# Dense + GELU, forward and backward, on one core: PSUM laid out by hand

## The chip, the cores and the metric

One Trainium2 chip, and of it one core. The metric is device time in microseconds of one execution, here of that core alone. The profiled execution is one run with the hardware profiler; its span runs from the first to the last instruction.

## The reference

```python
def _gelu(x): return jax.nn.gelu(x, approximate=True)
def _fwd_reference(x, w1, b1, w2, b2):         # x (1, 2048, 448), w1 (448, 1792), w2 (1792, 448), all bf16
    h = jnp.einsum("bsd,df->bsf", x, w1) + b1
    h = _gelu(h)
    return jnp.einsum("bsf,fd->bsd", h, w2) + b2
def reference(x, w1, b1, w2, b2, grad_out):
    _out, _vjp = jax.vjp(_fwd_reference, x, w1, b1, w2, b2)
    return (_out, *_vjp(grad_out))             # out, and the gradients of x, w1, b1, w2, b2
```

With u = x w1 + b1, h = gelu(u), q = grad_out w2^T and gh = q * gelu'(u), the six results are h w2 + b2, gh w1^T, x^T gh, the sum of gh over the rows, h^T grad_out, and the sum of grad_out over the rows.

## The kernel before

The 2048 rows are cut into NB = 4 blocks of SB = 512 rows, and the 1792 columns of the hidden layer into 14 f-tiles of 128, taken in NPAIR = 7 pairs. A step is one pair of f-tiles in one block, and there are NSTEP = 28. All of the order is written out by hand: inside `tc.manual_schedule()` every engine runs its instructions in the order of the program text, and the framework adds the semaphores and gives each tile its memory.

For a step f, TensorE computes u (transposed: 128 hidden columns by 512 rows) for the pair's two halves a = 0 and 1. Each half is three matmuls with 128 rows of contraction (`pe_u_fulls`, L201) and a "tail" with the 64 rows left over (`u_tail`, L217). `copy_u` (L256 on ScalarE, L258 on VectorE) adds the bias and copies each half from PSUM to the SBUF tile U4. Only the first, `copy_u(0, "av")`, splits the halves between ScalarE and VectorE; all others have both halves on ScalarE. Then follow, on 1024 columns of U4 at once, `act_gelu` (L262), `act_square` (L265), `dve_cubic` (L269, L270), `act_tanh` (L274) and `dve_gate` (L278 to L285). q of a step k is made in the same way (`q_tail` L224, then `pe_q_fulls` L247), and `dve_gh` (L290) multiplies it by the gate out of PSUM, both halves in one instruction.

What fills TensorE between u and q are "units": a unit is one tile of 128 rows of the output (kind "o", from hT) or of the gradient of x (kind "x", from ghT). A unit sums 7 pieces of two matmuls each (L322) in one PSUM bank, as far as the steps have come; `pieces(budget, ...)` issues them in the order in which units were opened. A finished unit is copied to a staging tile `st` (L333 on ScalarE or L335 on VectorE) and stored by GpSimd's queue (L336). There are STG = 5 staging tiles, so the sixth copy waits until the first store has landed.

The stages, in the order of time:

- steps 0 to 7, one at a time: u runs LEAD = 2 steps ahead of q. Four units are open from the start, a fifth and sixth from i = 6;
- steps 8 to 27, two at a time (the loop over n, nq = 10): u of steps k+2 and k+3, q of k and k+1, and one new unit (n < 2) or two (n from 2 to 8);
- the ten units that are left, in five pairs;
- the gradients of w1 (`ps_w`, L553 and L564) and of w2 (`ps_v`, L585), each a sum over 16 matmuls, with the sums for b1 and b2 on VectorE.

PSUM has eight banks of 512 floats per partition. The kernel before has two pools, psa and psb, each with two tiles of two banks that are given out in turn. In steps 0 to 7, u is always in one psa tile and q in the other (u of step 1 alone is where q comes next), and the units are in psb. From step 8 u has both psa tiles, q both psb tiles, and a unit takes half of one of these tiles, the other half being left empty:

```python
PU[f] = psa.tile([P, 2, SB], F32, name="pu", tag="pa")        # L198
in_a = k < NSINGLE or k >= NSTEP - 2                          # L211, NSINGLE = 8
PQ[k] = (psa if in_a else psb).tile([P, 2, SB], F32, name="pq", tag="pa" if in_a else "pb")
open_pair(psa, "pa", 1)                                       # L466, one unit in a psa tile
if n >= 2: open_pair(psb, "pb", 1)                            # L468, one unit in a psb tile
```

A tile is given out again when every access to the old one is over.

Of the kernel before, what the change touches and what calls it, by code (L numbers as in the profile page):

```python
# [9 lines left out]
ACT = mybir.ActivationFunctionType  # L10
# [9 lines left out]
def kernel(  # L20
# [42 lines left out]

    const = ctx.enter_context(tc.tile_pool(name="const", bufs=1))
    dram = ctx.enter_context(tc.tile_pool(name="dram", bufs=1, space=bass.MemoryType.DRAM))
    psa = ctx.enter_context(tc.tile_pool(name="psa", bufs=2, space=bass.MemoryType.PSUM))
    psb = ctx.enter_context(tc.tile_pool(name="psb", bufs=2, space=bass.MemoryType.PSUM))
    blk = ctx.enter_context(tc.tile_pool(name="blk", bufs=2))
    tmp = ctx.enter_context(tc.tile_pool(name="tmp", bufs=2))
    stg = ctx.enter_context(tc.tile_pool(name="stg", bufs=STG))  # L70
# [15 lines left out]
    gh_nat = const.tile([P, NB, NF, SPB, P], BF16, name="gh_nat")  # L86

    sched = ctx.enter_context(tc.manual_schedule())

    xT, gT = {}, {}  # L90

# [67 lines left out]
    nc.sync.dma_start_transpose(out=w1T_sb[:], in_=w1[:, :])  # L159
    load_g(1)  # L160

    pw = psb.tile([P, 2, SB], F32, name="pw", tag="pb")
    for i in range(9):
        nc.tensor.matmul(pw[:, 0, :], lhsT=zero[:, 0:P], rhs=zero[:], start=True, stop=True)
    for c in range(P // 32):
# [2 lines left out]

    hT, ghT = {}, {}
    PU, PQ = {}, {}  # L170
    U4 = [tmp.tile([P, 4, SB], BF16, name="U4", tag="U4", bufs=1)]
    A4 = [tmp.tile([P, 4, SB], BF16, name="A4", tag="A4", bufs=2) for _ in range(2)]
    Z4 = [tmp.tile([P, 4, SB], BF16, name="Z4", tag="Z4", bufs=1)]
# [20 lines left out]
    def pe_u_fulls(f):  # L194
        b, p = divmod(f, NPAIR)
        if p == 0:
            hT[b] = blk.tile([P, NF, SB], BF16, name="hT", tag="hT")
        PU[f] = psa.tile([P, 2, SB], F32, name="pu", tag="pa")  # L198
        for a in range(2):
            for kt in range(KF):  # L200
                nc.tensor.matmul(PU[f][:, a, :], lhsT=w1_f[:, kt, cols(p, a)], rhs=xT[b][:, kt, :], start=(kt == 0), stop=False,  # L201
                                 skip_group_check=True)

    def half(up):
# [2 lines left out]
    def open_q(k):  # L207
        b, p = divmod(k, NPAIR)
        if p == 0:
            ghT[b] = blk.tile([P, NF, SB], BF16, name="ghT", tag="ghT")  # L210
        in_a = k < NSINGLE or k >= NSTEP - 2  # L211
        PQ[k] = (psa if in_a else psb).tile([P, 2, SB], F32, name="pq", tag="pa" if in_a else "pb")

    def u_tail(f, a):
        b, p = divmod(f, NPAIR)
        hf = half(b not in WIDE)
        nc.tensor.matmul(PU[f][:, a, :], lhsT=wt1[hf, cols(p, a)], rhs=xT[b][hf, KF, :], start=False, stop=True,  # L217
                         tile_position=(hf.start, 0), skip_group_check=True)

    def q_tail(k, a, swap=False):  # L220
# [29 lines left out]
    def copy_u(f, engines):  # L250
        p = f % NPAIR
        for a in range(2):
            bias = b1T[:, 2 * FP[p] + a:2 * FP[p] + a + 1]
            dst = part(U4, [f])[:, a, :]
            if engines[a] == "a":
                nc.scalar.activation(out=dst, in_=PU[f][:, a, :], func=ACT.Identity, bias=bias)  # L256
            else:
                nc.vector.tensor_scalar(out=dst, in0=PU[f][:, a, :], scalar1=bias, scalar2=None, op0=ALU.add)  # L258

    def act_gelu(fs):  # L260
        for r in runs(fs):
# [47 lines left out]
    class Unit:  # L309
# [9 lines left out]
        def emit(self, p):  # L319
            src, w = (hT, w2_sb) if self.kind == "o" else (ghT, w1T_sb)  # L320
            for a in range(2):
                nc.tensor.matmul(self.ps[:, 0:D], lhsT=src[self.b][:, 2 * p + a, self.j * P:(self.j + 1) * P],  # L322
                                 rhs=w[:, 2 * FP[p] + a, :], start=(p == 0 and a == 0),
                                 stop=(p == NPAIR - 1 and a == 1 and not self.b2_pe), skip_group_check=True)
            if p == NPAIR - 1 and self.b2_pe:
                nc.tensor.matmul(self.ps[:, 0:D], lhsT=row0[:], rhs=b2_bc[:], start=False, stop=True, skip_group_check=True)
            self.done += 1

        def evict(self):
            st = stg.tile([P, SB], BF16, name="st", tag="st")  # L330
            r = ROW0[self.b] + self.j * P
            if self.by_act:
                nc.scalar.copy(out=st[:, 0:D], in_=self.ps[:, 0:D])  # L333
            else:
                nc.vector.tensor_tensor(out=st[:, 0:D], in0=self.ps[:, 0:D], in1=b2_bc[:], op=ALU.add)  # L335
            nc.gpsimd.dma_start(out=(out2 if self.kind == "o" else gx2)[r:r + P, :], in_=st[:, 0:D])  # L336

    todo = []
# [2 lines left out]
        todo += [Unit("x", b, j) for j in range(SPB)]  # L341
    open_units, finished = [], []

    def open_pair(pool, tag, n=2):
        t = pool.tile([P, 2, SB], F32, name="ps", tag=tag)
        for h in range(n):
            un = todo.pop(0)
            un.ps = t[:, h, :]
            open_units.append(un)

    def pieces(budget, fmax, gmax):
        for un in list(open_units):
# [43 lines left out]
    act_gelu([1])  # L396
    pe_u_fulls(2)
    pe_tails([2], [])
    open_pair(psb, "pb")
    open_pair(psb, "pb")  # L400
    pieces(4, 0, -1)
    pe_tails([], [0])
    pe_q_fulls(0)
# [8 lines left out]
    for i in range(1, NSINGLE):  # L412
        f = i + LEAD
        pe_u_fulls(f)
        pe_tails([f], [i])
        pe_q_fulls(i)
        if i > 1:
            act_tanh([i])
        evictions(2)
        copy_u(f, "aa")  # L420
        evictions()
        act_gelu([f])
        act_square([f])
        if i == 1:
            dve_gate([i])
            dve_cubic([i + 1])
        else:
            dve_cubic([i + 1])
            dve_gate([i])
        dve_gh(i)  # L430
        if i == 6:
            open_pair(psb, "pb")
        if i >= 5:
            stores(2, f - 1, i)
        traffic(i)
        pieces(7 if i >= 6 else 5, f - 1, i - 1)
# [3 lines left out]
    for n in range(nq):  # L440
        i = NSINGLE + n
        k = NSINGLE + 2 * n
        fs = [k + 2, k + 3] if k + 2 < NSTEP else []
        for f in fs:
            pe_u_fulls(f)
        pe_tails(fs, [k, k + 1])
        pe_q_fulls(k)
        pe_q_fulls(k + 1)
        if n == 0:
            evictions()  # L450
            act_tanh([k])
            for f in fs:
                copy_u(f, "aa")
            dve_gate([k])
            dve_cubic([k + 1])
            dve_gh(k)
            act_tanh([k + 1])
            dve_gate([k + 1])
            dve_gh(k + 1)
        else:  # L460
            for f in fs:
                copy_u(f, "aa")
            dve_gh(k)
            dve_gh(k + 1)
        if fs:
            open_pair(psa, "pa", 1)  # L466
            if n >= 2:
                open_pair(psb, "pb", 1)  # L468
            pieces(28, k + 1, k - 1)
            act_square(fs)  # L470
            if n < 2:
                evictions()
            act_gelu(fs)
            dve_cubic(fs)
            evictions(1)
            act_tanh(fs)
            dve_gate(fs, evictions)
        if i == 15:
            g_low = const.tile([P, SB], BF16, name="g_low")
            nc.gpsimd.dma_start(out=g_low[DL:P, :], in_=gT[3][0:DL, 0, :])  # L480
        stores(3, k + 1)
        traffic(i)
    stores(NSTEP, NSTEP - 1)
    flip = 1
    while todo:
        open_pair(psa if flip == 0 else psb, "pa" if flip == 0 else "pb")
        flip = 1 - flip
        pieces(28, NSTEP, NSTEP)
        evictions()

# [14 lines left out]
    for ft in range(4):  # L505
        load_h(ft)

    nev = [0]

    def gst(shape, f32src, dst, eng):  # L510
        st = stg.tile([P, SB], BF16, name="st", tag="st")
        return st

    def f_at(slot):
        return (2 * FP[slot // 2] + slot % 2) * P
# [31 lines left out]
                    nc.gpsimd.dma_start(out=v1[:, 0:2 * P], in_=gb1_w[0:1, F - 2 * P:F])  # L547

    def gw1_full(ft0, n, kt):
        ps = psb.tile([P, 2, SB], F32, name="ps_w", tag="pb")[:, 0, :]  # L550
        for st_ in range(NS):
            b, j = PLACE[st_]
            nc.tensor.matmul(ps[:, 0:n * P], lhsT=x_nat[:, st_, kt * P:(kt + 1) * P], rhs=gh_nat[:, b, ft0:ft0 + n, j, :],  # L553
                             start=(st_ == 0), stop=(st_ == NS - 1))
        o = stg.tile([P, SB], BF16, name="st", tag="st")
        nc.scalar.copy(out=o[:, 0:n * P], in_=ps[:, 0:n * P])
        nc.scalar.dma_start(out=out_2[kt * P:(kt + 1) * P, f_at(ft0):f_at(ft0) + n * P], in_=o[:, 0:n * P])

    def gw1_tail(ft0, n):
        ps = psb.tile([P, 2, SB], F32, name="ps_w", tag="pb")[:, 0, :]  # L560
        for st_ in range(NS):
            b, j = PLACE[st_]
            for h in range(2):
# [16 lines left out]
    def gw2_tile(ft, halves):  # L580
        w = D // halves
        for h in range(halves):
            ps = psa.tile([P, 2, SB], F32, name="ps_v", tag="pa")[:, 0, :]
            for st_ in range(NS):
                nc.tensor.matmul(ps[:, 0:w], lhsT=h_nat[ft][:, st_, :], rhs=g_nat[:, st_, h * w:(h + 1) * w],  # L585
                                 start=(st_ == 0), stop=(st_ == NS - 1))
            o = stg.tile([P, SB], BF16, name="st", tag="st")
            nc.scalar.copy(out=o[:, 0:w], in_=ps[:, 0:w])  # L588
            nc.scalar.dma_start(out=out_4[ft * P:(ft + 1) * P, h * w:(h + 1) * w], in_=o[:, 0:w])
# [44 lines left out]
```

## Time and profile before

| | |
|---|---|
| median of 3 runs | 278.41 us (276.49 to 278.45) |
| the profiled execution | 278.24 us, span 276.4 us, so 1.8 us lie around the span |
| mean granted TensorE clock | 0.999 |
| TensorE busy | 268.9 us (97%) |
| VectorE busy | 176.9 us (64%) |
| ScalarE busy | 138.8 us (50%) |
| GpSimd busy | 58.4 us (21%) |

The busy share of an engine is an average over stages with different limits, and the ends of matmuls are modelled, so a busy TensorE can still be one that has slack. "idle before, with a releaser" says what an engine waited for in front of an instruction. Names in the rows leave buffer numbers out: `pu` is u in PSUM, `U` the tile U4, `pq` is q in PSUM, `ps` a unit.

### The profile page before, as it was taken

What the parts mean: (1) busy time and instruction counts of PE and PEld (TensorE: products, weight loads), DVE (VectorE), ACT (ScalarE), POOL (GpSimd) and SP (SyncE); (2) the same over time, 40 slices, a digit from 0 to 9 for tenths busy, and PEclk for the clock granted to TensorE, in tenths of its full rate; (3) what the DMA queues carried; (4) which work ended last, traced back from release to release, by engine and by line L of the source; (5) the groups of instructions that cost most, each with busy time, mean ns of one, the idle gap of its engine ahead of it and who ended that gap; (6) DMA issues with size and microseconds to landing.
All of it is one profiled execution on the core that took longest, in us unless ns stands there. A gap on an engine that the chain in (4) does not pass through costs nothing.

```text
span 276.4 us, 3637 instructions
## 1 busy us (share of the span) xinstructions
PE 268.9 (97%) x1405; PEld 127.1 (46%) x1405; DVE 176.9 (64%) x213; ACT 138.8 (50%) x164; POOL 58.4 (21%) x77
## 2 busy tenths in 40 slices
PE   7999999999799999999999999999999999999995
PEld 2234434444344344444444445554444475555554
DVE  2388989969999997696977960207999993000000
ACT  2499979877898749696585901012111111112111
POOL 1000002542040221302114041311340006910000
PEclk9999999999999999999999999999999999999999
DMA  8999799999999954542445569998110111899951
GB/s 188 221 223 230 122 249 212 115 265 185 143 249 250 220 113 125 153 92 96 94 122 125 136 196 290 369 201 205 40 41 25 41 56 24 188 199 227 222 128 33
DMA packets 107521, 44.31 MB, mean 160 GB/s; under 512 B 91984, under 2 KB 104608, under 8 KB 107504
## 3 DMA queue, kind: packets, MB, share of 16 engines
q1 hardware_dynamic: 98224, 28.86, 55.0%
q0 software_dynamic: 4032, 11.55, 13.8%
q10 hardware_dynamic: 5248, 3.67, 4.4%
q8 instruction: 11, 0.18, 0.3%
q14 instruction: 6, 0.05, 0.1%
HBM read 7.23 MB, written 14.23 MB: 78 GB/s over the span
## 4 chain that ended last, share of the span: by engine, by line
PE 74%; DVE 14%; ACT 7%; DMA 2%; issue 2%; DVEq 0%
PE ps L322 24%; PE ps_v L585 15%; PE ps_w L553 13%; PE pq L247 8%; PE pu L201 8%; DVE ghT L290 3%; PE pu L217 3%; ACT U L256 2%; PE ps_w L564 2%; DVE Z L270 2%; ACT A L265 2%; DVE A L280 2%; DMA xT<-in_x_dram 2%; ACT hT L262 2%; DVE Z L285 2%
## 5 line engine op out<-in xcount | busy, mean ns | idle before, releaser
L256 ACT ACTIVATE U<-pu,b1T 128x512 bf16<-128x512 f32 x55 | 33.8, 685 | 26.7 <-PE pu L217 26.7
L322 PE MATMUL ps<-w1T_sb,ghT 128*128 128x448 bf16 x224 | 43.8, 352 | 1.6 <-ACT U L256 1.6
L322 PE MATMUL ps<-w_sb,hT 128*128 128x448 bf16 x224 | 44.8, 353 | 0.1
L585 PE MATMUL ps_v<-g_nat,h_nat 128*128 128x448 bf16 (+1 forms) x240 | 42.6, 340 | 0.0
L201 PE MATMUL pu<-xT,w_f 128*128 128x512 bf16 x168 | 40.6, 388 | 0.8 <-DMA xT<-in_x_dram 0.8
L290 DVE SCALAR_TENSOR_TENSOR ghT<-Z,pq 128x1024 bf16<-128x1024 bf16 x28 | 33.9, 1220 | 10.7 <-PE pq L247 9.2
L247 PE MATMUL pq<-gT,w2T 128*128 128x512 bf16 x168 | 39.4, 380 | 0.0
L336 POOL DMA_DIRECT2D out_dram<-st x32 | 18.2, 572 | 97.3 <-ACT st L333 50.0
L553 PE MATMUL ps_w<-gh_nat,x_nat 128*128 128x512 bf16 (+1 forms) x192 | 36.7, 352 | 0.0
L322 PEld LDWEIGHTS <-ghT 128*128 128x128 bf16 x224 | 21.9, 98 | 22.7 <-issue 1.9
L585 PEld LDWEIGHTS <-h_nat 128*128 128x128 bf16 x240 | 23.3, 98 | 19.3 <-issue 0.3
L322 PEld LDWEIGHTS <-hT 128*128 128x128 bf16 x224 | 21.8, 98 | 21.5 <-ACT hT L262 1.0
L274 ACT ACTIVATE Z<-Z 128x1024 bf16<-128x1024 bf16 (+1 forms) x19 | 27.7, 1457 | 6.6 <-DVE Z L270 6.6
L539 DVE TENSOR_TENSOR acc<-acc,gh_nat 128x1792 f32<-128x1792 f32 x14 | 30.0, 2142 | 0.5
L299 POOL DMA_DIRECT2D hT_dram<-hT x28 | 20.2, 726 | 46.5 <-DVE Z L269 44.6
L265 ACT ACTIVATE A<-U 128x1024 bf16<-128x1024 bf16 (+1 forms) x19 | 27.7, 1455 | 1.1 <-DVE U L258 0.8
L262 ACT ACTIVATE hT<-U 128x1024 bf16<-128x1024 bf16 (+1 forms) x20 | 27.7, 1391 | 0.2
L553 PEld LDWEIGHTS <-x_nat 128*128 128x128 bf16 x192 | 18.7, 98 | 17.8 <-issue 0.4
L201 PEld LDWEIGHTS <-w_f 128*128 128x128 bf16 x168 | 16.5, 99 | 21.7 <-issue 3.9
L247 PEld LDWEIGHTS <-w2T 128*128 128x128 bf16 x168 | 15.0, 98 | 23.2 <-issue 7.6
L588 ACT CAST st<-ps_v 128x448 bf16<-128x448 f32 (+1 forms) x15 | 7.6, 507 | 34.8 <-PE ps_v L585 34.8
L333 ACT CAST st<-ps 128x448 bf16<-128x448 f32 x20 | 10.0, 527 | 29.1 <-PE ps L322 28.0
(46 smaller groups left out, 204.2 us busy)
## 6 DMA issues: line engine op xcount, KB each, us to landing
hT_dram<-hT POOLq DMA_DIRECT2D x28, 256.0 KB, 4.1
out_dram<-st POOLq DMA_DIRECT2D x32, 112.0 KB, 4.3
x_nat<-in_x_dram SPq DMA_DIRECT2D x1, 1792.0 KB, 8.6
g_nat<-in_grad_out_dram SPq DMA_DIRECT2D x1, 1792.0 KB, 13.6
out_dram<-st ACTq DMA_DIRECT2D x13, 112.0 KB, 3.3
out_dram<-st ACTq DMA_DIRECT2D x9, 128.0 KB, 1.7
w_sb<-in_w_dram SPq DMA_DIRECT2D x5, 224.0 KB, 3.9
w_f<-in_w_dram SPq DMA_DIRECT2D x5, 192.0 KB, 4.1
```

The source lines that it names most:

```text
L201: nc.tensor.matmul(PU[f][:, a, :], lhsT=w1_f[:, kt, cols(p, a)], rhs=xT[b][:, kt, :], start=(kt == 0), stop=False, skip_group_check=True)
L247: nc.tensor.matmul(PQ[k][:, a, :], lhsT=w2T[:, kt, cols(p, a)], rhs=gT[b][:, kt, :], start=False, stop=(kt == KF), skip_group_check=True)
L256: nc.scalar.activation(out=dst, in_=PU[f][:, a, :], func=ACT.Identity, bias=bias)
L262: nc.scalar.activation(out=rows(hT, r), in_=part(U4, r), func=ACT.Gelu_apprx_tanh)
L265: nc.scalar.activation(out=part(A4, ks), in_=part(U4, ks), func=ACT.Square, scale=math.sqrt(3.0 * GELU_A * GELU_C))
L274: nc.scalar.activation(out=z, in_=z, func=ACT.Tanh, scale=-1.0 / 3.0)
L290: gates[k] = nc.vector.scalar_tensor_tensor(out=rows(ghT, [k]), in0=part(Z4, [k]), scalar=1.0, in1=PQ[k][:], op0=ALU.add, op1=ALU.mult)
L299: st = nc.gpsimd.dma_start(out=hT_dram_v[:, 2 * FP[p]:2 * FP[p] + 2, ROW0[b]:ROW0[b] + SB], in_=rows(hT, [f]))
L322: nc.tensor.matmul(self.ps[:, 0:D], lhsT=src[self.b][:, 2 * p + a, self.j * P:(self.j + 1) * P], rhs=w[:, 2 * FP[p] + a, :], start=(p == 0 ...
L539: nc.vector.tensor_tensor(out=v, in0=in0, in1=gh_nat[:, b, :, j, :], op=ALU.add)
L553: nc.tensor.matmul(ps[:, 0:n * P], lhsT=x_nat[:, st_, kt * P:(kt + 1) * P], rhs=gh_nat[:, b, ft0:ft0 + n, j, :], start=(st_ == 0), stop=(s ...
L585: nc.tensor.matmul(ps[:, 0:w], lhsT=h_nat[ft][:, st_, :], rhs=g_nat[:, st_, h * w:(h + 1) * w], start=(st_ == 0), stop=(st_ == NS - 1))
```

## The change

The two pools become one pool with eight banks under names of their own. `one_bank(n)` gives one of four single-bank tiles; `two_banks(n)` gives one of two tiles of two banks. The two halves of u are now two separate tiles. In steps 0 to 9 they have the banks 0 and 1 (step 1: 2 and 3). From step 10 the list `order_a` says which two banks the even step and which two the odd step takes. A unit that is opened beside u gets the bank `order_a[0]`, that of the first half of the even step, and the list is turned by one. q has `two_banks(0)` in steps 0 to 7 and after that the two tiles in turn (`order_b`); the second unit of n = 2 to 7 takes half of the tile that `order_b[0]` names, as before. At n = 8 the second unit is in a single bank, and q of steps 26 and 27 stays in the two-bank tiles. Units 2 and 3 have the single banks 2 and 3, behind u of step 1. The ten last units are in the four single banks. `ps_w` alternates between the two-bank tiles, and `ps_v` goes through the four single banks. No arithmetic is changed, and no instruction but for its tile.

```diff
-    psa = ctx.enter_context(tc.tile_pool(name="psa", bufs=2, space=bass.MemoryType.PSUM))
-    psb = ctx.enter_context(tc.tile_pool(name="psb", bufs=2, space=bass.MemoryType.PSUM))
+    psum = ctx.enter_context(tc.tile_pool(name="psum", bufs=1, space=bass.MemoryType.PSUM))
+    def one_bank(n, name):
+        return psum.tile([P, SB], F32, name=name, tag=f"one{n}")
+    def two_banks(n, name):
+        return psum.tile([P, 2, SB], F32, name=name, tag=f"two{n}")
...
-    pw = psb.tile([P, 2, SB], F32, name="pw", tag="pb")
+    pw = two_banks(1, "pw")
+    order_a, order_b = [0, 1, 2, 3], [0, 1]
...
-        PU[f] = psa.tile([P, 2, SB], F32, name="pu", tag="pa")
+        banks = (2, 3) if f == 1 else (0, 1) if f < NSINGLE + LEAD else order_a[2 * (f % 2):2 * (f % 2) + 2]
+        PU[f] = [one_bank(n, "pu") for n in banks]
         for a in range(2):
             for kt in range(KF):
-                nc.tensor.matmul(PU[f][:, a, :], ...
+                nc.tensor.matmul(PU[f][a][:], ...
...
-        in_a = k < NSINGLE or k >= NSTEP - 2
-        PQ[k] = (psa if in_a else psb).tile([P, 2, SB], F32, name="pq", tag="pa" if in_a else "pb")
+        PQ[k] = two_banks(0 if k < NSINGLE else order_b[k % 2], "pq")
...
-                nc.scalar.activation(out=dst, in_=PU[f][:, a, :], func=ACT.Identity, bias=bias)
+                nc.scalar.activation(out=dst, in_=PU[f][a][:], func=ACT.Identity, bias=bias)
             else:
-                nc.vector.tensor_scalar(out=dst, in0=PU[f][:, a, :], scalar1=bias, ...
+                nc.vector.tensor_scalar(out=dst, in0=PU[f][a][:], scalar1=bias, ...
...
+    def open_one():
+        open_unit(one_bank(order_a[0], "ps")[:, 0:D])
+        order_a.append(order_a.pop(0))
+    def open_two(n, units):
+        t = two_banks(n, "ps")
+        for h in range(units):
+            open_unit(t[:, h, 0:D])
...
-    open_pair(psb, "pb")
-    open_pair(psb, "pb")
+    open_two(1, 2)
+    for n in (2, 3):
+        open_unit(one_bank(n, "ps")[:, 0:D])
...
         if i == 6:
-            open_pair(psb, "pb")
+            open_two(1, 2)
...
-            open_pair(psa, "pa", 1)
-            if n >= 2:
-                open_pair(psb, "pb", 1)
+            open_one()
+            if n == nq - 2:
+                open_one()
+            elif n >= 2:
+                open_two(order_b[0], 1)
+                order_b.reverse()
...
     while todo:
-        open_pair(psa if flip == 0 else psb, "pa" if flip == 0 else "pb")
-        flip = 1 - flip
+        open_one()
+        open_one()
...
+    def bank_w():
+        flips[0] += 1
+        return two_banks(flips[0] % 2, "ps_w")[:, 0, :]
+    def bank_v():
+        order_a.append(order_a.pop(0))
+        return one_bank(order_a[-1], "ps_v")
```

More of the change, by code (lines that the diff above doesn't have):

```diff
@@ L197, in pe_u_fulls @@
             hT[b] = blk.tile([P, NF, SB], BF16, name="hT", tag="hT")
-        PU[f] = psa.tile([P, 2, SB], F32, name="pu", tag="pa")
+        banks = (2, 3) if f == 1 else (0, 1) if f < NSINGLE + LEAD else order_a[2 * (f % 2):2 * (f % 2) + 2]
+        PU[f] = [one_bank(n, "pu") for n in banks]
         for a in range(2):
             for kt in range(KF):
-                nc.tensor.matmul(PU[f][:, a, :], lhsT=w1_f[:, kt, cols(p, a)], rhs=xT[b][:, kt, :], start=(kt == 0), stop=False,
+                nc.tensor.matmul(PU[f][a][:], lhsT=w1_f[:, kt, cols(p, a)], rhs=xT[b][:, kt, :], start=(kt == 0), stop=False,
                                  skip_group_check=True)
@@ L216, in u_tail @@
         hf = half(b not in WIDE)
-        nc.tensor.matmul(PU[f][:, a, :], lhsT=wt1[hf, cols(p, a)], rhs=xT[b][hf, KF, :], start=False, stop=True,
+        nc.tensor.matmul(PU[f][a][:], lhsT=wt1[hf, cols(p, a)], rhs=xT[b][hf, KF, :], start=False, stop=True,
                          tile_position=(hf.start, 0), skip_group_check=True)
@@ L255, in copy_u @@
             if engines[a] == "a":
-                nc.scalar.activation(out=dst, in_=PU[f][:, a, :], func=ACT.Identity, bias=bias)
+                nc.scalar.activation(out=dst, in_=PU[f][a][:], func=ACT.Identity, bias=bias)
             else:
-                nc.vector.tensor_scalar(out=dst, in0=PU[f][:, a, :], scalar1=bias, scalar2=None, op0=ALU.add)
+                nc.vector.tensor_scalar(out=dst, in0=PU[f][a][:], scalar1=bias, scalar2=None, op0=ALU.add)
     def act_gelu(fs):
@@ L321, in emit @@
             for a in range(2):
-                nc.tensor.matmul(self.ps[:, 0:D], lhsT=src[self.b][:, 2 * p + a, self.j * P:(self.j + 1) * P],
+                nc.tensor.matmul(self.ps, lhsT=src[self.b][:, 2 * p + a, self.j * P:(self.j + 1) * P],
                                  rhs=w[:, 2 * FP[p] + a, :], start=(p == 0 and a == 0),
@@ L325, in emit @@
             if p == NPAIR - 1 and self.b2_pe:
-                nc.tensor.matmul(self.ps[:, 0:D], lhsT=row0[:], rhs=b2_bc[:], start=False, stop=True, skip_group_check=True)
+                nc.tensor.matmul(self.ps, lhsT=row0[:], rhs=b2_bc[:], start=False, stop=True, skip_group_check=True)
             self.done += 1
@@ L332, in evict @@
             if self.by_act:
-                nc.scalar.copy(out=st[:, 0:D], in_=self.ps[:, 0:D])
+                nc.scalar.copy(out=st[:, 0:D], in_=self.ps)
             else:
-                nc.vector.tensor_tensor(out=st[:, 0:D], in0=self.ps[:, 0:D], in1=b2_bc[:], op=ALU.add)
+                nc.vector.tensor_tensor(out=st[:, 0:D], in0=self.ps, in1=b2_bc[:], op=ALU.add)
             nc.gpsimd.dma_start(out=(out2 if self.kind == "o" else gx2)[r:r + P, :], in_=st[:, 0:D])
@@ L342, with open_unit @@
     open_units, finished = [], []
[L344 to L349, printed above, removed]
+    def open_unit(ps):
+        un = todo.pop(0)
+        un.ps = ps
+        open_units.append(un)
+    def open_one():
[5 more added lines that the diff above has]
+            open_unit(t[:, h, 0:D])
     def pieces(budget, fmax, gmax):
@@ L483 @@
     stores(NSTEP, NSTEP - 1)
-    flip = 1
     while todo:
-        open_pair(psa if flip == 0 else psb, "pa" if flip == 0 else "pb")
-        flip = 1 - flip
+        open_one()
+        open_one()
         pieces(28, NSTEP, NSTEP)
@@ L506 @@
         load_h(ft)
[L508 to L512, printed above, removed]
+    flips = [0]
+    def bank_w():
[4 more added lines that the diff above has]
+        return one_bank(order_a[-1], "ps_v")
     def f_at(slot):
@@ L549, in gw1_full @@
     def gw1_full(ft0, n, kt):
-        ps = psb.tile([P, 2, SB], F32, name="ps_w", tag="pb")[:, 0, :]
+        ps = bank_w()
         for st_ in range(NS):
@@ L559, in gw1_tail @@
     def gw1_tail(ft0, n):
-        ps = psb.tile([P, 2, SB], F32, name="ps_w", tag="pb")[:, 0, :]
+        ps = bank_w()
         for st_ in range(NS):
@@ L582, in gw2_tile @@
         for h in range(halves):
-            ps = psa.tile([P, 2, SB], F32, name="ps_v", tag="pa")[:, 0, :]
+            ps = bank_v()
             for st_ in range(NS):
```

## The prediction

> **What bounds the kernel now.** I read first the busy time by stage, then the chain of work that ended last, then TensorE's waits, then the timelines of ScalarE and VectorE at the places where the chain changes engine. The table by stage (window, length, then busy us of PE, PEld, DVE, ACT and POOL, clock, DMA share, GB/s):
>
> ```profile
> 25.00:40.40 15.40, 15.35 (x76) 6.17 (x75) 14.42 (x24) 13.51 (x16) 0.00 (x0) 1.00 0.94 190
> 59.60:92.20 32.60, 30.63 (x156) 13.47 (x152) 30.21 (x37) 26.18 (x26) 8.07 (x12) 1.00 1.19 206
> 92.20:161.80 69.60, 69.60 (x360) 31.90 (x360) 57.90 (x64) 50.28 (x49) 18.21 (x29) 1.00 0.51 124
> 161.80:188.30 26.50, 26.50 (x141) 13.70 (x140) 4.06 (x7) 1.94 (x5) 5.32 (x10) 1.00 1.05 280
> ```
>
> From 92.2 us on TensorE has no gap at all: matmuls of 512 columns follow each other at 0.216 us (12 in 2.59) and of 448 columns at 0.189 us (28 in 5.30), at a clock of 1.00. A new PSUM layout cannot shorten that; the end is the time at which TensorE gets going at 92.2, plus 184 us. So the question is what sets 92.2. The chain:
>
> ```profile
> 59.42 0.23 PE pu L217
> ...
> 59.67 0.45 ACT U L256
> ...
> 62.12 0.70 DVE Z L270
> ...
> 91.52 0.63 DVE st L335
> 92.15 0.04 issue
> 92.19 0.37 PE pq L224
> ```
>
> q of step 15 waits at 92.19 for VectorE to copy out a unit. VectorE reaches that copy after 30.2 busy us in the 32.6 from 59.6 on, in its own order: from 62.12 it has hardly a gap. 62.12 follows from ScalarE's four copies of u (steps 10 and 11), these from ScalarE's tanh and TensorE's u at 59.6. TensorE has run without a gap there since 40.41, when `dve_gh` of step 4 (39.13 to 40.35) freed q's only tile. And `dve_gh` ends a VectorE chain (14.42 of 15.40 us busy) that goes back to 24.95, where VectorE waited for ScalarE's square. From there back to the first copies of u at 9.7 the chain is ScalarE's, with short pieces of VectorE in it. So 9.7 to 25 is ScalarE's, 25 to 40 VectorE's, 40 to 59 TensorE's, 62 to 92 VectorE's. TensorE's own waits are few:
>
> ```profile
> PE ps L322 <- ACT U L256: 1.6, 1, 1.6
> PE pq L224 <- ACT U L256: 0.6, 1, 0.6
> PE pq L224 <- DVE st L335: 0.3, 1, 0.3
> ```
>
> **Part 1: the halves of u become tiles of their own.** The rows that decide are at the start:
>
> ```profile
> 8.65 1.03 PE L217 MATMUL pu<-xT,wt 64*128 64x512 bf16 x2
> 9.71 0.69 ACT L256 ACTIVATE U<-pu,b1T 128x512 bf16<-128x512 f32 x1 [6.42 <-PE pu L217]
> 10.43 0.75 DVE L258 TENSOR_SCALAR U<-pu,b1T 128x512 bf16<-128x512 f32 x1 [3.54 <-ACT U L256]
> 11.22 1.06 ACT L265 ACTIVATE A<-U 128x1024 bf16<-128x1024 bf16 x1 [0.82 <-DVE U L258]
> ```
>
> VectorE's copy of half 1 needs nothing of ScalarE's copy of half 0, yet waits for it, and ScalarE's begins only when both tails are over (9.68). Later copies show the same: at step 4 the tails start at 25.46 and 25.68, the second ends at 25.68 + 0.38 = 26.06, and the copy of half 0 starts at 26.10. So a wait holds for the whole two-bank tile, and with two tiles it goes: ScalarE can copy after the first tail, VectorE at 9.71 beside it, ending at 10.46 instead of 11.18. The square starts 0.72 earlier, and all of ScalarE's chain behind it. Bounds: 0 if VectorE still waits, 0.72 if the two read side by side at the durations above. For the latter: ScalarE's four copies at 91.75, beside a VectorE copy out of PSUM, took 2.42 us, against 2.40 at 72.00 without one. I take 0.72.
>
> The Trainium skill bears on this: page "PSUM — Partial Sum Buffer", section "PSUM bank collisions raise a hardware error", says that two engines on one bank collide, readers too, while different banks run clean. By that rule the two copies may overlap, which agrees with the 2.42 us beside 2.40; if two banks collided as well, they would have to stay in turn and the sum below would lose its 0.72.
>
> Does the 0.72 survive? VectorE at 24.95 waited 0.90 us for the square, so it follows. From 25 to 55 it is limited by itself and by q's tile, whose number is unchanged; the weights it needs come in time (the last transposes of the first block are issued at 21.56 and take 7.0 us to land, needed at 35). `dve_gh` of step 4 then ends at 39.6 and TensorE's stretch of 40 to 59 moves along.
>
> At 56 to 60 there is a second limit:
>
> ```profile
> 58.13 0.53 ACT L333 CAST st<-ps 128x448 bf16<-128x448 f32 x1 [1.05 <-DMA out_dram<-st]
> 58.55 1.06 ACT L274 ACTIVATE Z<-Z 128x1024 bf16<-128x1024 bf16 x1
> 59.67 2.42 ACT L256 ACTIVATE U<-pu,b1T 128x512 bf16<-128x512 f32 x4
> ```
>
> The sixth unit's copy waits for the store of the first (issued by GpSimd from 48.08 on, up to 10.3 us to landing, DMA engines saturated), the tanh is queued behind it on ScalarE, and the copies of u behind the tanh. The store is issued behind `dve_gh` of step 5, so its issue moves by 0.72 too; its landing moves by 0 (if the other transfers set it) to 0.72. In the first case the tanh still ends at 59.61 and the copies come only 0.05 earlier; at best they start when the first tail is over, 59.03 + 0.39 - 0.72 = 58.70, 0.95 earlier. Since GpSimd's queue is issued in order and moves as a whole, I take 0.7. VectorE's 62.12 moves by this, and with it 92.19.
>
> **Part 2: the unit in the bank of half 0.** At 71.66 TensorE waits 1.64 us for both copies of step 12 (ScalarE, four copies from 72.00 at 0.6 each: the second ends at 73.2). With a bank of its own the unit waits for one copy, and starts 0.6 earlier. But what is late next is the copy at 91.52, and VectorE does not get there sooner by it: TensorE would wait 0.6 longer at q of step 15, which has the same tile as before. Worth 0; worth 0.6 if VectorE were free. The next u needs the unit's bank only as its last half, 3 matmuls (0.65 us) later than before: slack only.
>
> **Part 3: units 2 and 3 behind u of step 1.** This adds a wait. Their first pieces, 4 matmuls of 0.19, ran at 13.5 to 15.1, ahead of the copies of step 1 (14.55 to 15.70), and q of step 0 waited for the copies at 15.76. Now the second and third pair of pieces wait for a copy each, and the tails and fulls of q (step 0) and all else on TensorE are queued behind: 2 x 0.19 = 0.38 us later against the copies. Cover: TensorE waits again 0.2 us at 17.8, VectorE has 0.90 us free at 24.95. Cost 0; 0.38 if that cover is gone. Since the copies come 0.72 earlier, q comes 0.34 earlier in all.
>
> **Part 4: the rest.** q of steps 26 and 27 now waits for `dve_gh` of 24 and 25, over at 154.5, and is due at 158.47: 4 us of cover. `ps_w` alternates as before; `ps_v` has four banks instead of two, but TensorE never waits there. A wait that is already met costs TensorE nothing that the rows show: u of two steps with two waits takes 12 x 0.216 + 0.10 = 2.69 us up to its tails, of one step with one wait 6 x 0.216 + 0.10 = 1.39. Instructions removed or added: none on the engines.
>
> **Sum**, against the profiled execution: 276.4 span + 1.84 around = 278.24; less 0.7 (Part 1), 0 (Parts 2 to 4) = **277.5 us**. That execution is within 0.2 us of the median of the runs shown, 278.41.
>
> **The rivals.**
> (A) *The store does not land earlier.* For: the DMA share is 1.17 from 40.4 to 59.6. Against: its issue is tied to VectorE. Then 278.24 - 0.05 = 278.2.
> (B) *The copies still take turns*, or slow each other down: the change does not do what it allows. For: nothing but that no row shows a ScalarE and a VectorE copy of one u side by side. With Part 3's 0.38 uncovered it would be 278.24 to 278.6.
> (C) *TensorE loses nearly all its waits for PSUM.* 1.64 + 0.59 at 15.76 + 0.33 at 92.19, and some 0.3 at 40.4, are 2.9: 275.3. The Trainium skill, page "Perfetto Trace Analysis", sections "Matmuls" and "Matmul Optimizations", says to rotate groups through different banks and to use all eight, which this change does where half-tiles stood empty. Against: 92.19 hangs on VectorE's 30.2 busy us, which no bank takes away.
> (D) *Slower: the last ten units run on two pairs of banks* instead of four tiles. A pair takes 5.3 us of TensorE; it is copied out right after (VectorE 172.41 and 177.76, ScalarE 167.11), and its banks are due again 5.3 us after its end, so 4 us are free. It decides once a copy is held by its staging tile for over 4 us: five tiles at 2 per 5.3 us tolerate stores of some 10.6 - 0.8 + 4 = 14 us to landing. The median there is 4.3 us, the longest of all stores 10.3, the DMA share 1.05. At 15 us and over, each of three pairs would wait 1 us or more: 278.24 + 3 = 281.2.
>
> **How the numbers follow.** Forecast 0.50; A 0.26; B 0.08; C 0.08; D 0.08. A measurement of this kernel can tell about 1% (2.8 us) from no change, and only C (faster) and D (slower) go beyond it: 0.08 faster, 0.84 within, 0.08 slower. The range leaves out C and D (0.16): its low end is the best of Part 1, 278.24 - 0.95 = 277.3, less 1.3 for the spread of the runs, whose lowest is 1.75 below this execution, so 276.0; its high end is B's 278.6 plus 0.3, 278.9.
>
> **What would show it.** Right: VectorE's first copy starts at about 9.7 beside ScalarE's, the first square at 10.5, `dve_gh` of step 4 ends near 39.6, the copies of step 10 start near 58.9, TensorE waits over 1 us at q of step 15, near 91.5, and then has no gap. TensorE's wait for a copy near 71 is about 1 us or less. Wrong: a VectorE wait that is gone between 62 and 92 (C), gaps of TensorE after 162 (D), or the sixth unit's copy still at 58.1 (A).

## The result, and the profile after

| | before | after |
|---|---|---|
| median of 22 runs each, on the same chip | 276.63 us (276.28 to 278.52) | **275.38 us** (275.05 to 277.52) |
| ratio after to before, 95% interval | | **0.9964** (0.9948 to 0.9979) |
| lower level: runs, median | 18, 276.53 us | 16, 275.33 us |
| upper level: runs, median | 4, 278.43 us | 6, 277.13 us |
| the profiled execution: time, span | 278.24, 276.4 us | 275.37, 273.6 us |

The change makes the kernel faster by 0.4%: 1.2 us at the lower level, 1.3 at the upper. The times of both kernels lie at two levels, 1.8 to 1.9 us apart, with nothing between them. Ratios and their intervals, here and below, are taken over the runs of both levels, which widens the intervals. The profiled execution of before is one of the upper level and that of after one of the lower, so their difference of 2.87 us is not what the change is worth. In what follows, times of a kernel are medians of its lower level unless something else is said.

The levels first, since every time stamp depends on them. The first lines of TensorE's timeline, before and then after (start and duration in us, the engine, the line, the operation, its tiles, how many):

```profile
1.18 4.02 PE L164 MATMUL pw<-zero 128*128 128x512 bf16 x9 [1.18 <-DVE zero L130]
6.00 2.72 PE L201 MATMUL pu<-xT,w_f 128*128 128x512 bf16 x6 [0.80 <-DMA xT<-in_x_dram]
...
9.61 1.47 PE L201 MATMUL pu<-xT,w_f 128*128 128x512 bf16 x6
```

```profile
1.18 3.99 PE L169 MATMUL pw<-zero 128*128 128x512 bf16 x9 [1.18 <-DVE zero L135]
6.05 1.46 PE L208 MATMUL pu<-xT,w_f 128*128 128x512 bf16 x6 [0.88 <-DMA xT<-in_x_dram]
7.43 0.60 PE L223 MATMUL pu<-xT,wt 64*128 64x512 bf16 x2
```

Both run nine idle matmuls at about 0.45 us each while they wait for x. After them the first u of the profiled run before still goes at 0.45 us per matmul (2.72 for six; the u of step 1, at 9.61, takes 1.47), that of after at 0.24. The granted clock in the table by stage reads 1.00 there in both, so the durations alone show it. The second tail is over at 9.68 in the one and at 8.03 in the other. Everything later hangs on that moment, so I call it E and compare the two traces relative to it:

| us after E | before | after | difference |
|---|---|---|---|
| first square (ScalarE) | 1.54 | 0.89 | -0.65 |
| copies of u of step 10 (ScalarE) | 49.99 | 49.05 | -0.94 |
| q of step 15 goes on (TensorE) | 82.51 | 81.33 | -1.18 |
| end of the span | 266.72 | 265.57 | -1.15 |

Of the 2.8 us between the spans, 1.65 are E and 1.15 are the change; the levels of the table above give 1.2 for the latter.

**The start.** From the timelines of ScalarE and VectorE of after:

```profile
7.86 0.69 ACT L262 ACTIVATE U<-pu,b1T 128x512 bf16<-128x512 f32 x1 [4.56 <-PE pu L223]
8.07 0.75 DVE L264 TENSOR_SCALAR U<-pu,b1T 128x512 bf16<-128x512 f32 x1 [1.14 <-PE pu L223]
8.92 1.06 ACT L271 ACTIVATE A<-U 128x1024 bf16<-128x1024 bf16 x1 [0.37 <-DVE U L264]
```

The two copies stand side by side, at the durations they had one after the other. ScalarE's begins at 7.86, after the first tail and before the second is over; VectorE's is released by TensorE (L223), no longer by ScalarE.

**Steps 10 and 11.** ScalarE's timeline of after:

```profile
54.17 0.97 ACT L339 CAST st<-ps 128x448 bf16<-128x448 f32 x2 [0.97 <-PE ps L328]
55.02 1.07 ACT L280 ACTIVATE Z<-Z 128x1024 bf16<-128x1024 bf16 x1
57.08 2.42 ACT L262 ACTIVATE U<-pu,b1T 128x512 bf16<-128x512 f32 x4 [0.99 <-PE pu L223]
```

Before, the fifth and the sixth unit's copies were 1.59 us apart, the tanh ended at 59.61 and the copies of u began at once. Now the two copies of units stand together, and ScalarE is idle for 0.99 us in front of the copies of u, which TensorE releases. That the two copies of units stand together is not the change's doing (see "The landing of the first store").

**The end of VectorE's stretch.** The chain of work that ended last, of after, then TensorE's waits for PSUM (in total, times, longest):

```profile
57.08 0.45 ACT U L262
...
59.53 0.69 DVE Z L276
...
88.69 0.63 DVE st L341
89.32 0.04 issue
89.36 0.37 PE pq L230
```

```profile
PE pq L230 <- DVE st L341: 0.8, 1, 0.8
PE ps L328 <- ACT U L262: 0.6, 1, 0.6
```

q of step 15 still waits for VectorE's copy-out, now 0.76 us where it was 0.33; in exchange the wait for copies of u near 70 is 0.6 instead of 1.64. Behind 89.36 TensorE has no gap, as before behind 92.19:

```profile
59.60:92.20 32.60, 31.23 (x155) 13.72 (x154) 31.03 (x36) 27.27 (x25) 8.67 (x12) 1.00 1.11 209
92.20:161.80 69.60, 69.60 (x363) 32.18 (x361) 57.03 (x63) 47.40 (x46) 17.24 (x27) 1.00 0.48 123
161.80:188.30 26.50, 26.50 (x140) 13.52 (x139) 5.20 (x9) 3.02 (x6) 5.43 (x10) 1.00 1.11 275
```

One gain between 49 and 81 us after E comes from no wait that the change took away. The first cubic of steps 10 and 11, on VectorE, before and then after:

```profile
67.97 0.93 DVE L269 TENSOR_SCALAR Z<-A 128x2048 bf16<-128x2048 bf16 x1
```

```profile
65.37 0.69 DVE L275 TENSOR_SCALAR Z<-A 128x2048 bf16<-128x2048 bf16 x1
```

It is the same instruction on the same shape, 0.24 us shorter, and it is the rest of the 1.18.

### The profile page after: what moved, and what is told of

Read it like the earlier page. It is cut to its first block, busy times and chain, and to the rows that moved or that the text cites. A ratio compares the mean times of both kernels' runs of the same rounds, so it can differ in the third digit from the quotient of the medians.

```text
span 273.6 us, 3642 instructions
## 1 busy us (share of the span) xinstructions
PE 267.0 (98%) x1405; PEld 126.7 (46%) x1405; DVE 176.8 (65%) x213; ACT 139.6 (51%) x164; POOL 58.8 (22%) x77
## 4 chain that ended last, share of the span: by engine, by line
PE 74%; DVE 16%; ACT 6%; DMA 2%; issue 1%; DVEq 0%; ACTq 0%
PE ps L328 24%; PE ps_v L605 16%; PE ps_w L573 13%; PE pq L253 8%; PE pu L208 7%; DVE ghT L296 4%; PE pu L223 2%; DVE A L286 2%; PE ps_w L584 2%; DVE Z L276 2%; ACT U L262 2%; DVE Z L291 2%; DMA xT<-in_x_dram 2%; ACT A L271 1%; DVE Z L275 1%
## 5 line engine op out<-in xcount | busy, mean ns | idle before, releaser
L208 PE MATMUL pu<-xT,w_f 128*128 128x512 bf16 x168 | 39.4, 379 | 0.9 <-DMA xT<-in_x_dram 0.9
```

Source lines behind the costliest of these rows:

```text
L208: nc.tensor.matmul(PU[f][a][:], lhsT=w1_f[:, kt, cols(p, a)], rhs=xT[b][:, kt, :], start=(kt == 0), stop=False, skip_group_check=True)
```

## The experiments

My theory after the result: nearly all of the 1.2 us comes from the waits of the copies of u for the whole two-bank tile. The rivals: the unit's own bank is worth something after all; the landing of the first store plays a part; the gain belongs to the start alone.

### The copies' waits put back

a1_turn takes the changed kernel and makes VectorE's first copy wait for ScalarE's:

```diff
+            if (f, a) == (0, 1):
+                tc.add_manual_dep(c.ins, copies[0, 0].ins.name, SYNC_DEP, reason="copies in turn")
```

> The changed kernel with one old wait put back: VectorE's copy of half 1 of step 0 again waits for ScalarE's copy of half 0; all other waits stay away. The changed kernel's common time is 275.35 us. Theory (the waits of the copies are what the change takes away): ScalarE copies from the first tail on for 0.69 us, VectorE then for 0.75, so the first square starts 0.43 us later than in the changed kernel (1.29 instead of 0.86 us after the second tail ends), and the whole comes 0.4 later, about 275.8. Rival (the gain lies in the units' own banks): 275.35, since VectorE has 0.6 us free in front of its third cubic. Rival (the gain is only a warmer TensorE clock in the profiled run): 275.35.

Measured: 275.69, 0.36 above after. VectorE's copy starts when ScalarE's ends:

```profile
8.49 0.75 DVE L265 TENSOR_SCALAR U<-pu,b1T 128x512 bf16<-128x512 f32 x1 [1.88 <-ACT U L263]
```

The first square comes 1.33 us after E instead of 0.89, the copies of step 10 at 49.49 instead of 49.05, q of step 15 at 81.82 instead of 81.33. So the 0.44 at the start arrives whole at q of step 15.

a2_tails adds to it that every copy of a half 0 waits for the second tail:

```diff
+            if a == 0:
+                tc.add_manual_dep(c.ins, tails[f, 1].ins.name, SYNC_DEP, reason="after both tails")
```

> The changed kernel with all old waits of the copies of u put back: in every step the copy of half 0 waits for the second tail as well, and in step 0 VectorE's copy waits for ScalarE's. The bank layout is that of the change. Theory: the first square starts 0.66 us later and the copies of step 10 another 0.2 to 0.25 later, so 275.35 + 0.9 = 276.25 of the 276.55 that the kernel before needs. Rival (the units' own banks): 275.35 to 275.5. If it comes out at 276.55, the copies' waits are all of the change.

Measured: 276.55, the time of before (276.50 on this chip), though the banks, the units and the order are those of the changed kernel. Relative to E its trace is that of before (square 1.54, copies of step 10 at 50.00, q of step 15 at 82.52). These waits are the whole of the change's worth; the 0.3 us that I had left to the units and the store are not there.

a4_before_aa goes the other way, from the kernel before: ScalarE makes both of the first copies, so that neither waits for an engine.

```diff
-    copy_u(0, "av")
+    copy_u(0, "aa")
```

> The kernel before, with both copies of step 0 on ScalarE, so that no copy waits across engines: the second half follows at 0.6 us instead of after ScalarE's 0.69 and then VectorE's 0.75. Theory: the first square starts 0.2 to 0.25 us earlier, and the time goes from 276.55 to 276.3, with the old layout. Rival (the units' own banks, or any part of the layout): 276.55.

Measured: 276.40 against 276.50, ratio 0.9984 (0.9958 to 1.001): not told apart by the times. In the trace the square comes 0.21 us earlier relative to E and q of step 15 0.26. By the trace, then, taking VectorE out of the first step would have given the kernel before a fifth of the gain; the times, 0.1 us apart, do not show it.

### The unit's own bank

a3_unit is the changed kernel with the unit opened beside u waiting for both copies of the even step, as the shared tile made it:

```diff
+                if p == 0 and a == 0 and self.after is not None:
+                    tc.add_manual_dep(m.ins, copies[self.after].ins.name, SYNC_DEP, reason="after both copies")
...
             open_one()
+            open_units[-1].after = (fs[0], 1)
```

> The changed kernel, but the unit that is opened beside u waits for both copies of the even step, as it did when it shared u's tile. Theory: TensorE's wait near 70 grows from 0.6 to 1.2 us, its wait at q of step 15 shrinks from 0.76 to about 0.15, and the time stays 275.35. Rival (the units' own banks): 0.6 us slower, 275.95, with the wait at step 15 unchanged.

Measured: 275.51 against 275.33, which is within the scatter of these runs (standard deviation 0.26), and q of step 15 at 81.35 us after E against 81.33. TensorE's waits:

```profile
PE ps L331 <- ACT U L263: 1.2, 1, 1.2
PE pq L231 <- DVE st L346: 0.3, 1, 0.3
```

What TensorE waits longer near 70 (1.2 for 0.6) it waits less at q of step 15 (0.3 for 0.8). A wait shortened by 0.6 us in front of an engine that waits anyway was worth nothing here.

### The landing of the first store

In the kernel before, the sixth unit's copy waited for the first store, and the trace names that DMA as what released it at 58.13. b3_before_stg6 gives the kernel before a sixth staging tile:

```diff
-    STG = 5
+    STG = 6
```

> The kernel before with six staging tiles instead of five, so that the sixth unit's copy does not wait for the first store. Theory (the copies of step 10 wait for the second tail, over at 59.63, as much as for the tanh, over at 59.61): the tanh comes up to 1 us earlier, the copies of step 10 do not, 276.5 as before. Rival (the store's landing was the limit at 58 to 60, as the prediction took it): copies of step 10 up to 0.2 us earlier and 276.3 or less.

Measured: 276.71 against 276.47, ratio 1.0008 (0.9997 to 1.0019). ScalarE's timeline:

```profile
54.81 0.97 ACT L333 CAST st<-ps 128x448 bf16<-128x448 f32 x2 [0.75 <-PE ps L322]
55.67 1.07 ACT L274 ACTIVATE Z<-Z 128x1024 bf16<-128x1024 bf16 x1
57.94 2.42 ACT L256 ACTIVATE U<-pu,b1T 128x512 bf16<-128x512 f32 x4 [1.20 <-PE pu L217]
```

There is no wait for the store, and the copies of u do not come sooner for it: ScalarE is idle for 1.20 us until the second tail is over, and the copies start 49.98 us after E, where before has 49.99. The sixth staging tile is not what took the wait away. With five tiles, a4_before_aa shows the same picture, and so does c3_before_evict; this is a4_before_aa:

```profile
54.82 0.97 ACT L333 CAST st<-ps 128x448 bf16<-128x448 f32 x2 [0.75 <-PE ps L322]
...
57.95 2.42 ACT L256 ACTIVATE U<-pu,b1T 128x512 bf16<-128x512 f32 x4 [1.20 <-PE pu L217]
```

The six stores took 9.9 us to landing (median) in the profile of before, 7.6 in that of a4_before_aa and 5.9 in that of c3_before_evict. So the wait at 58.13 belongs to one profiled execution and not to the layout, and even there it was level with the tails (tanh over at 59.61, second tail at 59.63). In the changed kernel the copy starts after the first tail, and in its profile the store has landed by then.

### VectorE's copy-out

b2_evict tests the statement that VectorE's order sets the start of TensorE's long stretch. In the changed kernel, at n = 2, the second copy-out of a unit is moved ahead of the gate:

```diff
-            evictions(1)
+            evictions(1 if n != 2 else NS)
```

> The changed kernel, with VectorE's second copy of a finished unit at n = 2 (88.69 in its profile) moved up right behind the first (85.50), ahead of three instructions of the gate. No work is added. Theory (VectorE's order decides when q of step 15 may start, and from there TensorE runs to the end without a gap): the wait of 0.76 us at q of step 15 goes, and the time falls by 0.7, to 274.6. Rival (TensorE or ScalarE is the limit there as well, or VectorE is late elsewhere by it): 275.3, no change, with a new wait behind it.

Measured: **274.22**, ratio to before 0.9915 (0.9902 to 0.9928), the fastest version; 1.1 us less than after on another chip (1.0 less than b1_warm11 below, which is after with two more idle matmuls, on the same chip), where 0.7 was expected. VectorE's and TensorE's timelines, first of after, then of b2_evict:

```profile
88.69 0.62 DVE L341 TENSOR_TENSOR st<-ps,b_bc 128x448 bf16<-128x448 f32 x1
...
87.78 0.39 PE L223 MATMUL pu<-xT,wt 64*128 64x512 bf16 x1
...
89.36 0.37 PE L230 MATMUL pq<-gT,w2T 64*128 64x512 bf16 x1 [0.76 <-DVE st L341]
...
89.88 2.76 PE L253 MATMUL pq<-gT,w2T 128*128 128x512 bf16 x12
```

```profile
85.31 1.15 DVE L341 TENSOR_TENSOR st<-ps,b_bc 128x448 bf16<-128x448 f32 x2
...
87.59 0.39 PE L223 MATMUL pu<-xT,wt 64*128 64x512 bf16 x1
...
88.56 2.76 PE L253 MATMUL pq<-gT,w2T 128*128 128x512 bf16 x11
```

From the first tail to the first of q's full matmuls it takes 0.97 us instead of 2.10. The wait of 0.76 is a part of it; the other 0.37 goes with the pairs: in b2_evict all tails of u and of q run side by side two by two (both start at 87.59), and in after the wait splits the third pair, so that a tail of u and later one of q run alone.

c3_before_evict makes the same move in the kernel before.

> The kernel before with the same copy-out moved ahead as in b2_evict. Theory: in the old layout VectorE and the waits for the banks are late by nearly the same amount at q of step 15, so taking VectorE's copy-out away there gains only the wait of TensorE seen at that place, 0.33 to 0.5: 276.5 becomes about 276.1; TensorE's wait of 1.64 near 71 stays. Rival: the move is worth the same in both layouts, 1.1: 275.4.

Measured: 275.95 against 276.46 on the same chip, 0.5 less, ratio 0.9984 (0.9959 to 1.0008). The interval, over both levels, does not exclude 1, but at the lower level the eight runs (275.65 to 276.05) all lie below all 20 of before (276.26 and more). As expected the move is worth half as much there, because in the old layout the next limit is close behind. TensorE's waits:

```profile
PE ps L322 <- ACT U L256: 1.6, 1, 1.6
...
PE pq L224 <- ACT U L256: 0.6, 1, 0.6
```

VectorE's 0.3 is gone from the list, the 1.6 near 72 remains, and the chain of work runs from ScalarE's two copies at 72.10 over TensorE alone to the end.

c4_evict_unit puts the units' wait of a3_unit into b2_evict.

> b2_evict with the unit waiting for both copies of the even step's u, as it did in the old layout. Theory: the unit's own bank was worth nothing in the change because VectorE's copy-out took the gain at q of step 15; with the copy-out out of the way it is worth its 0.6: 274.2 becomes 274.8, with TensorE's wait near 70 at 1.2 instead of 0.6. Rival: the units' wait is taken up again further on by the weights or the banks of q: 274.2 to 274.3.

Measured: 274.74, 0.52 above b2_evict's 274.22 (which ran on another chip; against before on its own chip the two gain 1.72 and 2.25). Against c2_evict_warm11 below, which is b2_evict with two more idle matmuls and ran on the same chip, it is 0.43, and so it is from E to the end of the span in the traces (264.88 and 264.45). TensorE's wait:

```profile
PE ps L331 <- ACT U L263: 1.2, 1, 1.2
```

So the unit's own bank is worth 0.4 to 0.5 us as soon as VectorE is out of the way, and nothing that the times show before that (a3_unit).

### The two levels

c1_warm2 has two idle matmuls instead of nine.

```diff
-    for i in range(9):
+    for i in range(2):
```

> The changed kernel with 2 instead of 9 idle matmuls ahead of the first u. Theory: the two levels of time, about 1.8 us apart, are the granted speed of TensorE at the first u. With 2 idle matmuls the first u's six matmuls take about 2.7 us (0.43 each) in the profile instead of 1.46, and the runs lie at the upper level, near 277.1, none near 275.3. Rival: the levels come from elsewhere (the first transfers); the time stays at 275.3 with some runs near 277.1, and the first u at 1.46.

Measured: all 12 runs between 276.57 and 277.44, median 276.98; none at 275.3.

```profile
5.97 2.72 PE L208 MATMUL pu<-xT,w_f 128*128 128x512 bf16 x6 [3.76 <-DMA xT<-in_x_dram]
```

The first u starts where it did, at about half the speed, and the time is that of the upper level. The 14 profiled executions of this document bear it out: in the four at the upper level (before, c1_warm2, c3_before_evict, c4_evict_unit) the six matmuls of the first u take 2.72 us, in the ten at the lower level 1.45 or 1.46. The upper level is a first u at half speed.

The other direction is weaker. b1_warm11 and b1_warm13 have 11 and 13 idle matmuls.

> The changed kernel with 11 instead of 9 idle matmuls on zeros at the start, which close the 0.9 us in which TensorE waits for x. The times of both kernels fall into two groups, 1.8 us apart; in the profile of the kernel before, from the upper group, the first u takes 2.72 us (0.43 per matmul), in that of the changed kernel, from the lower, 1.46. Theory (the groups are the TensorE clock at the first u): with no gap the clock is raised in time more often, and fewer of the runs lie near 277.1, none if the gap alone is to blame; the lower group stays at 275.3. Rival (the groups come from the transfers or from elsewhere): about a third of the runs at 277.1 as in the other kernels.

> The same with 13 idle matmuls. Where the clock is still low they end at about 6.8 us, 0.8 us after x has landed, so an upper group, if there is one, is smaller but the lower may rise by 0 to 0.7. Theory: no run at 277.1, or far fewer than one in three. Rival: one in three.

Measured: 275.22 and 275.71, five runs each, all at the lower level; but on that chip the kernels with nine idle matmuls (before, b2_evict, b3_before_stg6) had only one of 33 runs at the upper level, so these runs cannot tell.

c2_evict_warm11 has b2_evict's move and 11 idle matmuls.

> The changed kernel with VectorE's second copy-out of the query block moved ahead (as in b2_evict) and 11 instead of 9 idle matmuls. If the idle matmuls set the level of the time: all runs at b2_evict's 274.2, none near 276.0, though two more idle matmuls may put the first u some 0.2 later where x and w_f are there first (274.4). Rival: the two edits get in each other's way at the start, over 274.6.

Measured: 274.31, six of six at the lower level, while on the same chip three kernels with nine idle matmuls (before, c3_before_evict, c4_evict_unit) were at the upper level in 18 of 53 runs. If 11 changed nothing, six of six would come out 8 times in 100. That 11 keep the kernel at the lower level is likely, not shown; they cost nothing that these runs can tell (274.31 for 274.22).

## Why the prediction was right and wrong

The prediction said 277.5 us, 276.0 to 278.9; the result, 275.38, lies below the range. It gave 0.84 to a change within 1%, and that is what came (0.4%).

**The step that failed is the base of the sum.** It read "against the profiled execution: 276.4 span + 1.84 around = 278.24 ... within 0.2 us of the median of the runs shown, 278.41". Two of the three runs shown and the profiled one were at the upper level; 276.49 was at the lower, where 18 of 22 runs of before lie. The prediction took the 1.75 us between them for spread and kept 1.3 of it for its low end. The profile had the sign in it: six matmuls of the first u in 2.72 us, where the six of step 1 took 1.47. The same forecast from the lower level is 276.5 - 0.7 = 275.8. Of the 2.2 us between 277.5 and the lower level's 275.33, 1.7 are the base and 0.5 are Part 1.

Nine idle matmuls last 4.0 us, and the u behind them is sometimes fast and sometimes slow. The Trainium skill, page "TensorE: Matmul & The Clock Gate", section 'Part 1: The HAM clock gate (the "warmup" mystery)', says that full speed is granted after about 3.4 us of sustained work, counted in a window that runs freely, so that the moment varies from run to run. By that rule a first u that is fast in one run and slow in another was to be expected. The traces agree: behind the same nine idle matmuls the first u goes at 0.45 us per matmul in before (2.72 for six) and at 0.24 in a4_before_aa (1.45), though the granted clock of the table by stage does not show it. The window itself is seen in no run here.

**Part 1 was right in mechanism and short by 0.5.** At the start 0.72 was forecast and 0.65 measured. Rival B, copies that take turns or slow each other, did not come: they took 0.69 and 0.75 us side by side, as they had one after the other. That agrees with what the Trainium skill, page "PSUM — Partial Sum Buffer", section "PSUM bank collisions raise a hardware error", says of different banks. At 56 to 60 the prediction let the store's landing hold the gain at 0.7, with 0.95 as the best; 0.94 was measured. The store did not bind (b3_before_stg6), the wait for it is missing in other profiles with five staging tiles (a4_before_aa, c3_before_evict), and the copies of step 10 start after the first tail, as the bound of 0.95 had assumed. That is 0.24 of the miss. The other 0.24 is the shorter cubic, which the prediction did not have.

**Part 2 was right.** Worth 0, with TensorE's wait passed on to q of step 15 (a3_unit), "worth 0.6 if VectorE were free": 0.4 to 0.5 in c4_evict_unit. The wait at q of step 15 was forecast at over 1 us and came out at 0.76: VectorE reached its copy-out 0.24 us sooner than the copies of u alone would have let it, by the cubic.

**Parts 3 and 4** were put at 0, and the time shows nothing of them: with the copies' waits put back (a2_tails) all the rest of the new layout gives before's time within 0.1 us. The wait that Part 3 forecast is in the trace: the eight first pieces take 2.16 us, where they took 1.69, and q of step 0 starts 5.90 us after E, where it was 6.08, which is 0.18 earlier and not the 0.34 of the prediction. Its cover held: VectorE still waits 0.62 us for the square of step 3, where it waited 0.90.

**Rivals A, C and D.** A, a store that holds the copies back at 58, is out. C, 275.3, is nearest to the median by its number, and that is luck: its 2.9 us were taken from the upper level, and its mechanism did not come. TensorE's waits for PSUM behind the start fell from 2.6 us to 1.4, not to nearly nothing, and the wait at q of step 15 stayed, as the argument against C said. D, gaps with the last ten units, did not come: TensorE is busy for all of 161.80 to 188.30.

**What stays open.** The cubic of steps 10 and 11 takes 0.93 us in before, a2_tails, a4_before_aa, b3_before_stg6 and c3_before_evict, and 0.69 in after and all the kernels whose copies start after the first tail. So it goes with the change, and a2_tails shows that it goes with the copies' waits and not with the banks. It is no wait that the profile shows: VectorE begins the cubic 0.10 to 0.11 us after its instruction before in all 14 traces. Two things differ beside it. Where it takes 0.93 it begins 0.02 to 0.04 us after the first of TensorE's tails and after the end of ScalarE's gelu; where it takes 0.69 it begins 0.18 to 0.19 us ahead of the tails and 0.04 to 0.05 ahead of that end. No run was made to find out whether either is the cause.

## What to carry to other kernels

A tile of several PSUM banks is waited for as one: a reader of one bank waits for the writers of the other, and two engines that read it take turns, so where halves are copied on their own, make them tiles of their own. Before a sum is made against a profiled execution, ask whether the runs lie at more than one level and which one the profile shows; TensorE's first matmuls tell. A wait that is shortened in front of an engine that waits anyway is worth its length only after the other limit is moved, so such edits are to be priced together (the unit's bank: 0 alone, 0.4 to 0.5 us with VectorE's copy-out moved). A wait for a transfer that one profile shows may belong to that execution alone: look for it in a second profile before it becomes a term of the sum.

## What the runs showed of the hardware

- A slow start is carried whole through a kernel 275 us long: 1.26 us more for the first six matmuls and 0.43 more for the two tails, 1.7 (c1_warm2) to 1.9 us at the end. The granted clock in the table by stage does not record it.
- Matmuls of 64 rows of contraction on different halves of the array start together (both at 87.59 in b2_evict), so that eight tails take 0.97 us up to the next instruction; tails on the same half start one after the other (75.23, 75.45 and 75.67 in after). A wait in the middle of the pairs took 0.76 us for itself and 0.37 for the pair that it split.
- One VectorE instruction, the same on the same shape, took 0.93 us in five traces and 0.69 in nine. The cause is open.
